# A state-space, token-mixing and MLP kernel on one core: the same steps issued in another order

## The chip, the core and the metric

The kernel runs on one core of a Trainium2 chip. A core has five engines that run their own instruction streams in order and meet at semaphores: PE (TensorE, matmuls; its weight loads are listed apart as PEld), DVE (VectorE), ACT (ScalarE), POOL (GpSimd) and SP (SyncE, which here only issues DMAs). Sixteen DMA engines serve the core. The metric is the device time of one execution in microseconds, the median of several runs.

## The reference

With x of 2048 x 512, the output is x plus a long convolution gated by an MLP block. Both branches see the same normalised input.

```python
xn = _layernorm(x, axis=-1)
s = _A_ref(xn, A_A_re, ..., A_log_dt, A_Dskip)      # state-space convolution
g = _silu(_B_ref(xn, B_w1, B_w2, B_w3, B_w4))       # token mixing and MLP
return x + s * g

# _A_ref: a kernel of length 2048 for each of 512 channels, from 128 complex states,
# and the convolution with it by Fourier transforms
P = jnp.exp(logdA[:, :, None] * l[None, None, :])
K = jnp.einsum("dn,dnl,dn->dl", Cc, P, dB).real
Yf = Uf * Kf[None, :, :, :]
y = ... + u * Dskip[None, None, :]

# _B_ref: four quarters of the channels shifted by +1, -1, +2, -2 tokens, then the MLP
h = _gelu(_layernorm(x, axis=-1) @ w1)
hs = jnp.concatenate([g0, g1, g2, g3], axis=-1) @ w2
x1 = x + hs
h2 = _gelu(_layernorm(x1, axis=-1) @ w3) @ w4
return x1 + h2
```

The shapes are L = 2048, D = 512, 128 states and an inner MLP width F = 1376.

## The kernel before

**How the work is staged.** X stays on the chip as sixteen slices of 128 tokens x 512 channels. The stages, with the names of their tiles, are these.

- *Start.* X is loaded in five pieces (x0 is slices 0 and 1, x1 is 2 and 3, then three of four slices), each in four transfers by rows. 40 matmuls on the identity (`ident`) run while nothing else is there. DVE and ACT normalise X (`stats`, `mv`, `rs`, `bs`).
- *Token mixing.* Eight pairs of slices are normalised once more (`x2`), transposed (`xT`, on TensorE for the first four pairs, by a transposing DMA of float16 halves `x2h` for the rest), multiplied with w1 (`h_pair`, h0 to h7, into `pb`) and passed through gelu (`hT`). `hs_pair` multiplies with w2 and adds to X. The same X goes through the first step of the Fourier transform (`u_stage1`, `ue`), and its result to DRAM (`scr_Ud`).
- *Weights.* w3 and w4 are loaded twice (`wst`): once for a sum of squares that sets a scale, once to be split in two float16 halves (`w3h`, `w4h`).
- *Tables.* The convolution's kernel is built in sixteen chunks of 32 channels (`phases`, `waves`, `factors`, `sums`): magnitudes and phases by Exp and Sin on ACT, products on DVE (`wv`), 64 small matmuls (into `pc`), a copy `kev`, the first transform step (ks0 to ks15, copies `k1e`), and two stores to DRAM a chunk, `scr_Kfa` for chunks 0 to 7 and `scr_Kfb` for 8 to 15.
- *MLP.* Eight blocks of two slices, each in six pieces: matmuls with `w3h` (groups of 12, 128x256), gelu to `g`, split to float16 halves `ghl`, matmuls with `w4h` (groups of 6, 128x512). These groups have no deadline but the end, and the order uses them to fill TensorE while other chains run.
- *Products.* In two halves of the channels (0 and 1), each step loads matrices `cst`, the input's transform `uin` and the kernel's `kin`, multiplies spectra (kspec, uspec), and goes through the inverse step (inv) to `z1e` and DRAM (`scr_Zda`, `scr_Zdb`). The second half does this in eight steps, with float16 halves `kx` and `uh`; step n loads its `cst` into the buffer that step n-2 used. The loads read all of a scratch array, so they wait for its last store.
- *End.* Eight gates (Silu on X) and, for each half, eight inverse steps (`zin0.0` to `zin0.7`, `zin1.0` to `zin1.7`): load `zin`, matmuls into `pc` and `pd`, DVE multiplies them into X, adds the input `xr`, and stores. zin0.3 loads into the buffer of zin0.0, zin0.6 into that of zin0.3.

**What sets the order.** The functions do not issue anything. Every operation is recorded as a step with its dependencies (`Plan.add`, or `Plan.together` for a group of matmuls), 1952 in all. Then `Plan.order` reads a list that is written out in the source, `ORDER`, and `Plan.issue` emits the steps in it, all from one line (330), which is why every row of the profile has that line and is told apart by its tiles. Since each engine runs its stream in order, the list fixes the order on each engine, SP's DMA issues among them (some DMAs are issued by ACT, as the X loads and stores by rows). A step that is a plain copy or a scale and bias (`Either.copy`, `Either.affine`) may run on ACT or on DVE: its number then ends in `a` or `v`. There are 370 of these.

```python
def order(self):
    out = []
    for word in ORDER.split():
        op = self.ops[int(word.rstrip("av"))]
        op.eng = {"a": "ACT", "v": "DVE"}.get(word[-1]) or list(op.alts)[0]
        op.cost, op.calls = op.alts[op.eng]
        out.append(op)
    place = {op.idx: k for k, op in enumerate(out)}
    assert len(place) == len(out) == len(self.ops)
    assert all(place[d] < place[op.idx] for op in out for d in op.deps)
    return out
```

The compiler puts a load of a function set before an ACT operation whose function is not in the set that is loaded. In this kernel Exp, Sin, Gelu, Sqrt and Silu are in five sets, so the order on ACT also sets how often a set is loaded.

**Steps by number**, as they stand in the list: 5 to 8 are the loads of x0, 20 to 23 those of x1, 9 and 10 those of w1; 2 is the group of 40 identity matmuls; 142, 143, 145 and 146 are h0; 741 is ks7 and 1268 ks15; 849 and 1586 are the first spectrum products of either half; 1635, 1663, 1691, 1719, 1747 and 1775 load `cst` for steps 2 to 7 of the second half; 1799 is its last inverse and 1802 the last store to `scr_Zdb`; 1820 and 1841 are the matmuls of zin0.0 and zin0.3, 1840 the load between them; 1867 to 1869 are zin0.6; 1562 is the last MLP matmul group and 1563, 1564 its two updates of X.

Of the kernel before, what the change touches and what calls it, by code (L numbers as in the profile page):

```python
# [116 lines left out]
23 20 21 0 22 39 7 8 1 6 5 105 86 3 2 106 107 108 109 110 111 112 87 89 88 90 113 91 114 115a 92 93 94 95 25 24  # L117
26 27 116a 96 97a 1070 98v 117a 120v 99v 100 101a 102v 103 118 172 170 4 168 171 169 173 9 104a 10 19 18 11 28
166 167 174 175 176 121 123 124 177 178 122v 119a 125 145 44 179 180v 183v 146 46 126 127 128 181a 147 47 48
187a 208a 142 31 29 30 182v 129 78 205a 130 148 79a 153a 184v 228 229 230 131 143 160 185 35 34 33 32 132 232  # L120
133 149v 154a 231 144 186a 188 134 552 226 189a 233 193 150a 227 234 235 135 236 237 194 161 196 190 293 553 295
294 291 238 14 292 297 155 156 13 16 15 191 239 298 296 138a 240 299 244v 300 140a 301 202a 242a 302 141 554
241v 303 201a 49 245v 50 209 195 206 52 51 304 246a 247 53 54 192 152 17 151 380 382 203 249a 214 207a 250a 197a
198a 305 215 211 212 12 199 204 200 157 251 139 56 216 55 210a 59 45 80 217 243v 57 555 381 307a 272a 213 383 58
60 253 254 306a 81a 61 164 218a 62 36 252 223a 219a 384 248 308v 273v 222a 158 63 274 255 67 268v 162 68 64 256
257 220 225 259 276 221 224 275 565 277 314v 269a 69 270 70 136 137 71 557 258 65 261a 260a 279 265a 315v 278 66
264a 316 388 309v 72 280 282 73 271 337v 310a 311v 74 84 312 262 263 281 284v 283v 318 75 560 562 319 333v 317
266 267 338v 287a 76 339 313 288a 77 321 322 85v 334v 323 324 335 285 286 42 82 586 558 320 344 83a 345 556 385
559 566 567 340 326a 325a 289 346 389 336 341 290 330a 329v 43 37 328 327 568 359 360 587 561 347 588 331 349v
571 159 348v 40 332 163 353v 352v 350 351 361 375 378 446 374 570 448 390 342 355 569 377 572 449 563 564 362  # L130
354 41 363v 394 592 468 450 364a 589 438 591 386 590 391 470 471 396 439 574 573 440 343 576 575 387 443 454 577
578 595 593 165 441 579a 395 367a 397 392 356 376 357 456 455 400 402 607 393 594 404 608 442 358 366 398 457
580 472 581 582a 583a 597 459 584 403 596 613 372 609 401 447 368a 369 451 399 416 610 611 460 598 452 599 405
417 444 365 406 371 435 418 585 612 600a 628 370 616 629 458 630 469 473 419 474 601 38 407 475 453 462 432 614
631 633 632 480 495 602 420 408 603a 604a 461 615 409 634 421 410 445 411 379 499 476 605 606 657 412 618 422
413 477 617 478 414 373 482 423 637 424 479 425 494 481 463a 544a 635 433a 545a 464 415 619 620 502 621a 485
548a 549a 546 636 622 426 491 434 649 428 550 436a 650 496 659 660 547 465 466a 503 517 516 437 639 654 521 651
504 661 638 430 551 467 653 652 492a 746 623 747 488 489a 518 507 624a 490 662 748 510 493 655 513 749a 861 753
524 511a 750 754 760 512 761 755 756a 751 775 776 640 641 752 656 486 757 625a 767a 768a 427 769 514a 525a 663
515 527 526 664 528a 762 771a 763a 529 429 770 530 642a 533 764 500 643 683 777 782 758 531a 665 532 684 626 627  # L140
772a 773 783 784 534a 774 658 759 778a 779 789 765 766 644 780 796 797 685 535 668 483 666 671 667 669 670 790
785a 791a 786 645a 686 798 673 646a 792 688 672 687 803 689 505 781 804 846 648 692 810 787 674 675 704 676a 805
677 431 647 811 788 678 793 847 812 799a 817a 705 679a 690 806a 706 825 795 800 794 680a 707 818a 709 832 826
691 807 693 801 802 808 809 694 813a 814 821a 822a 695 696 713 681 819 708 823 827 828a 725 726 820 501 727 710
829 711 824 815 833 697a 834 698 839 816 728 835a 840 1273 830 1274 699 682 712 714 731 730 836 700a 841a 715
842 729 732 734 733 701a 1280 703 1281 831 837 838 716 1275 717 1282 1079 1071 1276v 718a 719 735 1277 1072 736
1302 1287 843 484 845 1294a 1081 1283a 702 844 1284 1080 1073 1076 720 721a 722a 724 723 1288 737 738 1278 1279
1285 1303 1075 1106 1082 1295a 1298a 739a 1296 1074 740 1077 1084 1083 1078 1085 487 1289 1304 1086 1290a 1291
741 851 1286 1305v 1299v 742a 743a 1107 1087 1088 1300 1093 1090 1089 1297 1316 1309 1310 497 1306 1292 1293
1307 1308 506 1108 1091 1092 1317 1311 1312a 1109 1111 744 1301 745 1330 1323 1331 1313 1095 1094 862 1112 508  # L150
1314 1318a 498 848 849 850a 852 1110 509 853 860 536 1096 1097 1324 854 855 1113 856 1315 1098a 857a 858a 865
863 1319 1325 1326a 1128 537 538 876 1114 1115 875 859 889 1332 864a 866 868 867 869 890 1320 1099 1327 1116
1117 539 1352 1337 1338 874 1100 870 871a 1101 872a 1102a 877 1103a 1344a 878a 1322 1321 873 888 904 879 903
1129 1105 1333a 1345a 1339 1130 1346 1347 880 1131 882 1118 881 883 1119 1353 1334 1104 1354 1134 1328 1329 1133
884 885a 1132 1335 1150 886v 1359 1137 1151 1340a 1152 891 893 917 1366 1336 1341 887 902 1135 1120a 1348a 1342
1360 1153 892a 894 1121 895 1349a 1155 1122 896 897 1355a 898 899a 900a 918 916 1136 1350 1123 905 1124a 906a
907 1343 1138 1125a 1154 1356 908 1357 901 909 911 910 1351 1139 1361 912 1140 1141 1367 913a 1126 919 1142a 931
1156 920a 914v 1157 1143 1159 930 915 1144 1362a 921 1172 922 1373 1374 1173 923 1358 1180 1174 924 1176 925
1158 1127 1177 1175 1368v 1369 1178 1179 926 932 927a 928a 1145 929 1182 933 1363 945 946 935 934a 936 937 939
938 1380 1381 1161 1364 1365 940 1370 1185 1183 1184 1375 1376a 1181 1194 1186 941a 1394v 1160 944 1146a 942a  # L160
1382 1387 947 943 949 1383a 948a 1147a 1187 950 1377 959 952 958 973 974 1388 1162 1163 1188 951 953 1389 1191
1395v 522 1371 1372 1207 954 1409 955a 956a 1396 1190 960 957 1384 1164a 1398a 1189 1148 972 1397 1208 961 963
962v 964 965 966 1209 1378 1402 1379 1390a 967 1165 1391 1403 1385 1166 968 1399a 1192 1193 1400 1149 969a 970a
988 1210 1167 975 976a 977 978 980 979 986 1410 1386 1168a 981 1169a 971 1170 1195 987 1001 1211 1212 1404 1405a
1196 1213 1392 1393 523 982 1197 1198 984a 991 983a 1401 1171 985 1000 1216 989 1199a 990a 1002 1406 1229 1230
1407 1416 1200 1201 1417 1408 992 993 1231 1430 995 1411 1431 1423 1424 1214 1412a 994 996 1235 1014 1232 1015
1418a 1016 1202 1215 1218 998a 1425 1413 1005 1217 997a 999 1203a 1204a 1432 1419 1238 1205 1003 1004a 1006 1008
1219 1220 1007 1251 1233 1234 1414 1009 1444v 1415 1010 1028 1012a 1011a 1013 1206 1252 1221v 1029 1452 1253
1017 1222 1236 1019 1420 1018a 1437 1020 1022 1021 1254 1223 1224 1256 1023 1426a 1024 1030 1422 1026a 1043
1025a 1237 1421 1027 1427 1225a 1226a 1240 1227 1044 1228 1239 1433a 1453 1438 1445a 1042 1033 1031 1032a 1057  # L170
1260 1446 1034 1255 1241 1242 1434 1035 1243a 1244 1036 1428 1245 1429 1257 1037 1439 1435 1246 1038 1058 1258
1259 1247a 1454 1248a 1448a 1040a 1447 1039a 1056 1459 1466 1261 1262 1440a 1250 1045 1047 1046v 1048 1041 1263
1264 1049 1441 1265a 1050 1051 1460 1449v 1266 1052 1267 1268 1450 1053a 1059 1249 1461 1054v 1269v 1270v 519
1060v 1061 1062 1436 1608 1580 1455a 1063 1456 1442 1443 1457 1064 1065 1451 1804 1055 1467 1610v 1271 1066
1067a 1458 1272 1582v 1565 1566 520 1462v 1567 1463 1568 1611 1583 1811 540 541 1473 1474 1569 1464 1480 1579
1570 1571 1465 1572 1573 1574 1576 1578 1581 1068a 1475 1577 1476a 542 1575 1468a 1584v 1609 1069 1481 1612a
1692 1607 1482 1637 1590 1585 1586 1636 1665 1469 1613 543 1664 1470 1587a 1487 1588a 1589v 1591 1592 1693 1471
1596 1600 1472 1597a 1598a 1477 1599a 1601 1483a 1602 1640a 1488 1593 1614 1595a 1484 1818 1615a 1594v 1616a
1617a 1618 1638a 1478 1641 1603 1813 1604a 1489 1619 1605v 1639 1635 1624 1625a 1626a 1628 1666a 1885 1627a
# [1179 lines left out]
```

## Time and profile before

| | |
|---|---|
| time, median of 3 runs | 536.88 us (535.10 to 538.08) |
| the profiled execution, its span | 536.6 us |
| granted TensorE clock, mean | 0.994 |
| instructions | 13619 |

The profile's times are those of one execution of 536.6 us. A windows row splits the span into stretches, and the stages stand in them roughly like this: start to 13 us, token mixing to 100, first tables and MLP to 248, first products, second tables and MLP to 380, the last tables to 421, second products, gates and first inverse steps to 518, and the end. A row of the timeline has the start, the busy time, the engine, the operation with output and inputs, the shapes, how many instructions are put together, and in brackets how long the engine stood idle before and what released it. In the chain of waits each row is start, length, and what the time was spent on.

### The profile page before, as it was taken

What the parts mean: (1) busy time and instruction counts of PE and PEld (TensorE: products, weight loads), DVE (VectorE), ACT (ScalarE), POOL (GpSimd) and SP (SyncE); (2) the same over time, 40 slices, a digit from 0 to 9 for tenths busy, and PEclk for the clock granted to TensorE, in tenths of its full rate; (3) what the DMA queues carried; (4) which work ended last, traced back from release to release, by engine and by line L of the source; (5) the groups of instructions that cost most, each with busy time, mean ns of one, the idle gap of its engine ahead of it and who ended that gap; (6) DMA issues with size and microseconds to landing.
All of it is one profiled execution on the core that took longest, in us unless ns stands there. A gap on an engine that the chain in (4) does not pass through costs nothing.

```text
span 536.6 us, 13619 instructions
## 1 busy us (share of the span) xinstructions
PE 516.5 (96%) x5628; PEld 332.4 (62%) x5628; DVE 489.8 (91%) x755; ACT 425.2 (79%) x692; POOL 0.7 (0%) x6
## 2 busy tenths in 40 slices
PE   8999999999999999999999999999899899999992
PEld 7787664554475766565765666575565667666631
DVE  4999999999999999999999999999877799997277
ACT  3999999899899999999799897868646566774340
POOL 0000000000000000000000000000000000000000
PEclk9999999999999999999999999999999999999997
DMA  8989975689677325356375738838889969896997
GB/s 228 214 268 257 230 200 155 190 132 127 158 188 118 46 36 60 42 68 112 120 137 148 150 108 167 145 94 176 149 170 169 348 201 297 261 280 226 314 277 205
DMA packets 212830, 93.50 MB, mean 174 GB/s; under 512 B 163297, under 2 KB 196065, under 8 KB 212385
## 3 DMA queue, kind: packets, MB, share of 16 engines
q1 hardware_dynamic: 208032, 88.18, 71.3%
q10 hardware_dynamic: 4736, 4.46, 2.8%
q8 instruction: 44, 0.72, 0.6%
q14 instruction: 18, 0.14, 0.1%
HBM read 56.96 MB, written 29.36 MB: 161 GB/s over the span
## 4 chain that ended last, share of the span: by engine, by line
PE 63%; DVE 12%; ACT 11%; DMA 7%; issue 3%; SPq 1%; DVEq 0%; ACTq 0%
PE pb L330 24%; PE pa L330 17%; PE pd L330 11%; PE pc L330 11%; DVE wv L330 4%; DMA scr_Kfb<-k1e 3%; DVE X L330 3%; ACT wv L330 2%; ACT mag L330 2%; ACT L330 2%; SPq L330 1%; DMA kin<-scr_Kfb 1%; DMA scr_Kfa<-k1e 1%; DMA cst<-c_gq 1%; ACT g L330 1%
## 5 line engine op out<-in xcount | busy, mean ns | idle before, releaser
L330 PE MATMUL pb<-x1T,w3h 128*128 128x256 f16 (+1 forms) x1056 | 125.1, 273 | 1.2 <-ACT g L330 1.2
L330 PE MATMUL pa<-w4h,ghl 128*128 128x512 f16 (+1 forms) x528 | 123.2, 380 | 0.0
L330 PEld LDWEIGHTS <-w3h 128*128 128x128 f16 (+1 forms) x1056 | 102.3, 100 | 27.8 <-issue 11.0
L330 PEld LDWEIGHTS <-ghl 128*128 128x128 f16 (+1 forms) x528 | 49.3, 98 | 59.1 <-issue 8.7
L330 ACT ACT_TABLE_LOAD x52 | 66.7, 1283 | 2.0 <-PEq L1347 1.2
L330 ACT ACTIVATE wv<-wv 128x2080 f32<-128x2080 int32 x32 | 63.0, 1968 | 0.3 <-DVE wv L330 0.3
L330 ACT ACTIVATE g<-pb,wsc 128x512 f32<-128x512 f32 (+1 forms) x48 | 30.6, 651 | 12.8 <-PE pb L330 11.5
L330 ACT ACTIVATE ghl<-g,wsc 128x512 f16<-128x512 f32 (+1 forms) x39 | 26.6, 688 | 13.3 <-PE pa L330 8.3
L330 DVE TENSOR_TENSOR wv<-wv,eg 128x2048 f32<-128x2048 f32 x16 | 36.5, 2284 | 0.1
L330 DVE TENSOR_TENSOR wv<-mag,wv 128x2048 f32<-128x2048 f32 x16 | 36.6, 2285 | 0.0
L330 PE MATMUL pd<-pr,cst 64*128 64x256 f32 x256 | 36.3, 402 | 0.0
L330 PEld LDWEIGHTS pc<-wv 128*32 128x32 f32 x2048 | 29.8, 109 | 9.7 <-issue 6.2
L330 PE MATMUL pc<-wv 128*32 128x64 f32 x2048 | 32.5, 220 | 2.7 <-issue 1.9
L330 DVE SCALAR_TENSOR_TENSOR ghl<-g,wsc,ghl 128x512 f16<-128x512 f32 (+1 forms) x48 | 33.5, 701 | 1.0 <-ACT ghl L330 0.8
L330 ACT ACTIVATE wv<-wv,halfpi 128x2080 f32<-128x2080 f32 x16 | 32.9, 2056 | 0.1
L330 ACT ACTIVATE mag<-par 128x128 f32<-128x128 f32 x132 | 32.8, 441 | 0.0
L330 ACT ACTIVATE kh<-pc,ksc 128x256 f32<-128x256 f32 (+1 forms) x40 | 20.1, 553 | 14.1 <-PE pc L330 12.5
L330 PEld LDWEIGHTS pd<-pr,cst 64*128 64x128 f32 x256 | 22.0, 186 | 11.5 <-issue 8.3
L330 PE MATMUL pb<-xT,w 128*128 128x256 f32 x128 | 29.0, 382 | 0.0
L330 PEld LDWEIGHTS pb<-xT,w 128*128 128x128 f32 x128 | 23.8, 190 | 5.5 <-issue 1.6
L330 PE MATMUL pb<-w,hT 128*128 128x512 f32 x58 | 26.9, 599 | 0.0
L330 DVE BATCH_NORM_STATS2 stats<-X 128x6 f32<-128x512 f32 x32 | 21.4, 681 | 5.3 <-DMA X<-in_A_u_dram 5.3
(167 smaller groups left out, 882.7 us busy)
## 6 DMA issues: line engine op xcount, KB each, us to landing
wst<-in_B_w_dram SPq DMA_DIRECT2D x20, 512.0 KB, 4.0
scr_Ud<-ue SPq DMA_DIRECT2D x32, 256.0 KB, 3.2
scr_Kfa<-k1e SPq DMA_DIRECT2D x16, 256.0 KB, 6.2
uin<-scr_Ud SPq DMA_DIRECT2D x16, 256.0 KB, 4.1
cst<-c_gp SPq DMA_DIRECT2D x16, 256.0 KB, 3.5
kin<-scr_Kfa SPq DMA_DIRECT2D x16, 256.0 KB, 3.6
scr_Zda<-z1e SPq DMA_DIRECT2D x16, 256.0 KB, 3.0
scr_Kfb<-k1e SPq DMA_DIRECT2D x16, 256.0 KB, 6.0
```

The source lines that it names most:

```text
L330: ins = [getattr(self.engines[op.eng], name)(*args, **kw).ins for name, args, kw in op.calls]
```

## The change

Only the string `ORDER` differs: 82 of its lines are replaced by 78. It holds the same 1952 numbers, so the steps, their shapes, buffers and PSUM banks are the same; their place differs, and 116 of the 370 steps that may run on either engine change it, 59 from DVE to ACT and 57 from ACT to DVE. The beginning and the end of the two lists:

```diff
 ORDER = """
-23 20 21 0 22 39 7 8 1 6 5 105 86 3 2 106 107 108 109 110 111 112 87 89 88 90 113 91 114 115a 92 93 94 95 25 24
-26 27 116a 96 97a 1070 98v 117a 120v 99v 100 101a 102v 103 118 172 170 4 168 171 169 173 9 104a 10 19 18 11 28
...
-1867 1871 1861 1899 1862 1864 1563 1564 1868 1845 1869 1831 1810 1865 1872 1873 1896 1898 1846 1897 1900 1874
-1943 1909 1877 1875 1902 1901 1910 1911 1876 1878 1903 1863 1913 1922 1905 1907 1914 1915 1924 1923 1916 1904
-1906 1917 1919 1918 1920 1926 1935 1936 1937 1927 1928 1938 1940 1939 1941 1929 1942 1944 1945 1930 1931 1932
-1946 1947 1950 1951 1948 1933 1949
+0 7 3 2 5 8 6 89 23 87 88 19 44 90 91 92 93 22 20 21 105 107 94 95 108 96 98v 24 106 109 9 97a 110 39 99a 111 100 102v
+103 27 112 10 101a 113 114 115v 117v 118 104a 142 143 116a 119a 26 120v 121 86 25 170 123 124 1 166 172 125 4 126 34
...
+1828 1899 1563 1810 1896 1898 1871 1921 1847 1925 1897 1909 1872 1865 1873 1864 1943 1911 1874 1848 1875 1900 1902
+1878 1901 1913 1910 1903 1922 1924 1876 1914 1915 1926 1906 1907 1846 1923 1863 1935 1916 1862 1917 1927 1937 1877
+1919 1920 1905 1904 1936 1928 1944 1938 1942 1939 1940 1929 1941 1918 1930 1931 1933 1932 1946 1945 1947 1948 1949
+1950 1951
```

Counted in the two lists, in the stretches that are spoken of below:

| | before | after |
|---|---|---|
| x0's four loads | behind x1's four | ahead of them |
| MLP matmul groups ahead of table chunk 2 / 8 / 15 | 0 / 67 / 123 | 16 / 84 / 139 |
| MLP groups between ks7 and the first product of half 0 | 13 | 10 |
| MLP groups in the release of `cst` to its use, steps 2, 3, 4, 7 of half 1 | 3, 2, 2, 2 | 2, 2, 1, 1 |
| MLP groups between zin0.0 and zin0.3 | 5 | 3 |
| MLP groups between the last inverse of half 1 and zin1.0 | 21 | 11 |
| zin0.6's matmuls (1867) | behind the last MLP group (1562) | ahead of it |
| function-set loads on ACT | 52 | 57 |

More of the change, by code (lines that the diff above doesn't have):

```diff
@@ L122 @@
[L122 to L136, printed above, removed]
```

133 lines of the change are left out of this document (72 added, 61 removed).

## The prediction

> **What bounds the kernel now.** I read the page's first lines first, then the windows by stage, the list of what TensorE waited for, and last the rows of the places where it waited. The order alone changes, so the question is which waits a new order can remove, and which it makes.
>
> ```profile
> span 536.6 us, 13619 instructions
> PE 516.5 (96%) x5628; PEld 332.4 (62%) x5628; DVE 489.8 (91%) x755; ACT 425.2 (79%) x692; POOL 0.7 (0%) x6
> ```
> ```profile
> 100.00:248.00 148.00, 146.03 (x1643) 88.00 (x1641) 145.34 (x198) 140.23 (x225) 0.00 (x0) 1.00 0.64 107
> 248.00:380.00 132.00, 131.31 (x1666) 84.38 (x1669) 130.98 (x167) 111.24 (x180) 0.00 (x0) 1.00 0.62 136
> 380.00:421.00 41.00, 37.75 (x494) 23.51 (x483) 30.74 (x57) 22.86 (x34) 0.00 (x0) 1.00 1.03 195
> 421.00:518.00 97.00, 96.91 (x940) 63.95 (x937) 78.47 (x112) 59.62 (x98) 0.00 (x0) 1.00 0.88 272
> 518.00:536.60 18.60, 8.40 (x164) 2.83 (x162) 13.96 (x28) 1.06 (x1) 0.00 (x0) 0.83 0.76 211
> ```
> ```profile
> PE pc L330 <- issue: 1.9, 1, 1.9
> PE pc L330 <- DVE kx L330: 1.4, 2, 1.0
> PE pa L330 <- POOL ident masks.py:199: 1.4, 1, 1.4
> PE pd L330 <- DVE x L330: 1.3, 1, 1.3
> PE pb L330 <- ACT g L330: 1.2, 2, 0.7
> PE pc L330 <- ACT k1e L330: 0.9, 1, 0.9
> PE pc L330 <- DVE kev L330: 0.6, 1, 0.6
> ```
>
> The first fence is the page, the second the windows, the third what PE waited for (us in total, times, longest). A window row gives the stretch, its length, then busy time of PE, PEld, DVE, ACT and POOL, the granted clock, the DMA share and GB/s. TensorE (PE) is busy 516.5 of 536.6 us; the other 20.1 us are all there is to win, and some 10 of them are the tail from 518 on, where DVE finishes the output. TensorE's work is the same 1952 steps, so the floor is near 517 plus a start and a tail. DVE is as full as TensorE up to 380 (145.34 of 148, 130.98 of 132): its results come just in time. From 421 to 518 TensorE has no hole (96.91 of 97.0), while the DMA engines are busy 0.88 of the time. There anything that comes late is paid in full.
>
> **The change part by part.** Same steps; I count what stands between two steps in either list and price it by this profile's rows.
>
> Start, **-1.3**. The new list issues x0's four loads ahead of x1's four (the old one has them behind), so 512 KB less stand before the first transposes.
>
> ```profile
> 0.00:13.40 13.40, 10.78 (x80) 10.59 (x80) 6.25 (x27) 4.72 (x8) 0.70 (x6) 1.00 0.88 228
> ```
> ```profile
> 1.35 10.78 PE L330 MATMUL pa<-ident 128*128 128x128 f32 x80 [1.35 <-POOL ident masks.py:199]
> ...
> 13.45 1.09 PE L330 MATMUL pd<-ident,x 128*128 128x128 f32 x8 [1.31 <-DVE x L330]
> ```
>
> At 228 GB/s, 512 KB is 2.3 us. The transposes now start at 13.45; the warm-up matmuls on the same engine end at 1.35 + 10.78 = 12.13, so only 1.3 of the 2.3 count. Bounds: nothing (the normalisation on DVE and ACT then sets the start) to 2.4, if h0, which now follows three transposes and not four, also moves up.
>
> Waits in the first 380 us, **-1.0 and -2.7**. Around 66 us, ahead of the eighth projection (h7), the weight loads wait 1.9 us.
>
> ```profile
> PEld pd L330 <- ACT ue L330: 1.1, 2, 0.8
> PEld pc L330 <- DVE x2h L330: 0.8, 1, 0.8
> ```
>
> They wait for a chain from h3 through x2h and the transposing DMA to h7. TensorE work between its source and its use grows from 19.2 to 20.5 us: I take 1.0 off (0 to 1.9). In the table chunks the waits for k1e, kev and g are 0.9 + 0.6 + 1.2 = 2.7. The new list has far more MLP work ahead of each chunk's matmuls: groups of MLP matmuls ahead of chunk 2 go from 0 to 16, of chunk 8 from 67 to 84, of chunk 15 from 123 to 139. TensorE's work ahead of chunk 8, less DVE's work ahead of what it needs, goes from 248.3 - 240.0 to 273.7 - 253.9, from 8 to 20 us of lead. So all 2.7 goes. The other end is 0: the lead is real only if DVE isn't held up by the MLP's own halves.
>
> The hole of 1.9 marked "issue" waits for nothing the trace shows. I take half, **-0.9** (0 to 1.9).
>
> In the tail zin0.6's matmuls and its two multiplies move ahead of the last MLP update.
>
> ```profile
> 519.47 0.74 DVE L330 TENSOR_TENSOR X<-X,pd 128x256 f32<-128x256 f32 x2
> 519.59 1.06 ACT L330 ACTIVATE X<-X 128x1024 f32<-128x1024 f32 x1 [4.84 <-DVE X L330]
> ```
>
> DVE is the chain there: two multiplies (0.74) leave it, and those of zin1.0, which don't need the last Silu (1.06 on ACT), fill its wait. DVE's steps behind the update fall from 26 to 24, by such rows from 12.4 to 11.7 us: **-0.65** (0 to -1.2).
>
> Now what gets worse. **Last stage: the constants.** Each product step loads its matrices (cst, 512 KB) into a buffer that the inverse matmuls two steps before set free.
>
> ```profile
> 431.75 0.34 SPq L330 DMA_DIRECT2D cst<-c_gq  x1
> ...
> 437.21 0.58 PEld L330 LDWEIGHTS <-cst 128*64 128x64 f16 x12 [0.37 <-DMA cst<-c_gq]
> ```
> ```profile
> PEld L330 <- DMA cst<-c_gq: 0.9, 3, 0.4
> ```
> ```profile
> cst<-c_gq SPq DMA_DIRECT2D x1, 512.0 KB, 5.4
> ...
> cst<-c_gq SPq DMA_DIRECT2D x1, 512.0 KB, 3.6
> ```
> ```profile
> 422.57 1.31 PE pb L330 x12
> ```
>
> The loads for steps 2 to 7 landed after 5.4, 3.6, 4.9, 4.9, 4.5 and 3.6 us (the DMA view of each stretch; the first and the last of the six stand above). Between release and use the old list has 5.3 to 5.4 us of TensorE work, and the load was needed the moment it came (437.21 is 5.46 after 431.75): three of the six uses waited for it with their weight load, 0.9 in all. The new list has one MLP group of 12 matmuls (1.31) or one inverse fewer in four of them: 4.2, 4.2, 4.0, 5.4, 5.3 and 3.5 us. With 0.25 from release to issue and from landing to use, the stalls are 5.65 - 4.2, nothing, 5.15 - 4.0, nothing, nothing, 3.85 - 3.5: **+2.95**. Bounds: every load at 3.6 gives 0.35, every one at 5.4 gives 1.45 + 1.45 + 1.65 + 0.25 + 0.35 + 2.15 = 7.3. The Trainium skill, SBUF — State Buffer, section "The DMA setup-cost knee", fits a transfer by some 2 us and its bytes at 436 GB/s, an estimate of 3.2 us for 512 KB; no run here shows one under 3.5, and by it this term were nothing and the sum 2.95 lower.
>
> **zin0.3.** Its load takes the buffer that zin0.0's matmuls free; TensorE work between them falls from 7.2 to 4.8 us (two MLP groups fewer).
>
> ```profile
> zin<-scr_Zda SPq DMA_DIRECT2D x1, 512.0 KB, 3.5
> ```
> ```profile
> zin<-scr_Zda SPq DMA_DIRECT2D x7, 512.0 KB, 6.4
> ```
>
> At 3.5 us, this load's own, nothing is late; at 6.4, the median of seven in this stage, 1.85 is. The new place is nearer to the last scr_Zdb store and its reloads, so half: **+0.9**.
>
> **Turnarounds through DRAM.** Behind the first half's last table chunk (ks7) stand 10 MLP groups before its spectrum needs them, not 13: 13.1 us of cover, not 16.7. Behind ks15 the cover goes from 19.0 to 18.3.
>
> ```profile
> 400.96 0.13 DVE k1e L330
> ...
> 402.93 9.37 DMA scr_Kfb<-k1e
> ...
> 412.35 5.86 DMA kin<-scr_Kfb
> ```
> ```profile
> scr_Kfa<-k1e SPq DMA_DIRECT2D x16, 256.0 KB, 6.2
> kin<-scr_Kfa SPq DMA_DIRECT2D x16, 256.0 KB, 3.6
> ```
>
> For ks7 that is copies and issue 1.9 (400.96 to 402.93), store 6.2, load 0.5 + 3.6: 12.2, under 13.1; with the 9.37 and 5.86 of the other half 17.6, 4.5 over. I take **+1.0**, nearer to its own rows (0 to 4.5). ks15 waits today (kx, 1.4), so 0.7 less cover is **+0.7** (0 to 1.4). The losses sum to +5.55.
>
> **Engines and function sets.** 116 copies change engine (59 to ACT, 57 to DVE): no net work moves. Changes of the array's form between neighbouring matmuls fall from 188 to 182; none has a row of its own, and by the nearest, 12 weight loads in 0.58 at 437.21, six are worth 6 x 0.05: **-0.2** (0 to -0.3). With that the gains sum to -6.75. ACT's function-set loads, counted in the list, go from 52 to 57.
>
> ```profile
> L330 ACT ACT_TABLE_LOAD x52 | 66.7, 1283 | 2.0 <-PEq L1347 1.2
> ```
>
> That is 5 x 1.283 = 6.4 us more on an engine that idles 111 us: priced at nothing, with the lead above as cover.
>
> The stage from 421 also gets shorter for the same traffic: from its first product to the end TensorE's work falls from 106.2 to 85.2 us, and the lists' transfers only from 30.3 to 28.8 MB. At 272 GB/s (0.88 share, so some 309 at full share) that is 93 us in about 95. I charge no more than the two loads above, but it is why they may land late.
>
> **Sum.** -6.75 + 5.55 = -1.2, span 536.6 to 535.4. The median of the runs, 536.88, is 0.28 over the profiled span: **535.7**.
>
> **The rivals.**
> **A, faster**: the loads land as their fastest did (3.5 and 3.6) and the turnarounds stay covered. The losses shrink to 0.35: 536.88 - 6.75 + 0.35 = 530.5. For it: half of the load rows. Against: three loads at 4.9 and over, at a lower share of DMA than is to come. The page's rule above speaks for A.
> **B, slower**: the constants' loads all land at 5.4 and zin0.3's at 6.4, since the transfers of the last stage crowd. 7.3 + 1.85 + 1.0 + 0.7 - 6.75 = +4.1: 541.0; with ks7's 4.5 as well, 544.5. It decides at a mean landing of about 5.2 us: from there each 0.1 us costs 0.6, and the sum passes +2.7.
> **C, moved waits**: DVE, full to 380, doesn't run ahead as counted, and the waits of 2.7, 1.0 and 0.9 come back elsewhere: 535.7 + 4.6 = 540.3. For it: DVE at 98% in those windows. Against: the lists' lead.
> **D, function sets**: the five loads fall where TensorE waits for a g, as twice today (1.2 us), each in full: 535.7 + 6.4 = 542.1. For it: those two waits. Against: ACT's 111 us. The Trainium skill, ScalarE: Activation LUTs, section "What ACT_TABLE_LOAD costs", gives a load of 1283 ns, as the row does, and 1380 ns of draining besides, which would make 13.3 us of the five. The row's idle time, 2.0 us before 52 loads, doesn't show such a drain.
>
> **How the numbers follow.** Forecast 0.40 (its own range 533 to 538: one quarter of it under 534.2); A 0.26; C 0.12; B 0.18; D 0.04. A measurement of this kernel tells some 0.5%, 2.7 us, from no change: 534.2 to 539.6. Faster: 0.10 + 0.26 = 0.36. Same: 0.30 and parts of C (0.06) and B (0.04), 0.40. Slower: 0.06 + 0.14 + 0.04 = 0.24. The range runs from A's time, 530.5, to 542.0, between B's two times and about D's; it leaves out about 2 in 10.
>
> **What would show it.** Start: transposes at 12.1, no wait for x. Chunks: no wait for kev, k1e or g between 100 and 380, and chunk 8 standing further back in time. Last stage: in place of 96.91 of 97.0, TensorE waits for cst in four places and perhaps for zin; a wait named kin or for the spectrum's copies behind ks7. It is wrong if TensorE waits for DVE between 100 and 380 as much as today, if cst lands in under 4 us throughout (A), or if a wait appears in the weight preparation or for ACT behind a function-set load.

## The result and the profile after

The changed kernel is **slower**: 563.21 us (median, 558.40 to 566.49) against 537.48 for the kernel before (with a fourth run added to the three above), a ratio of 1.046 (95% interval 1.040 to 1.053). The forecast was 535.7 with a range to 542.0, so even the range missed it, by 21 us.

The page of the changed kernel (its steps are all issued from line 326):

```profile
span 561.9 us, 13611 instructions
...
PE 524.5 (93%) x5628; PEld 337.7 (60%) x5628; DVE 494.2 (88%) x753; ACT 431.4 (77%) x699; POOL 0.7 (0%) x6
```

TensorE does the same 5628 matmuls in 8.0 us more (524.5 for 516.5) and is not busy for 37.4 us, where it was 20.1. The sum is the 25.3 us by which the span grew. To find where, I split both executions at one event: the issue of the last store of the last table chunk, ks15 (402.9 us before, 428.9 after). The windows of the kernel before, then of the changed one (length, then busy PE, PEld, DVE, ACT, POOL, granted clock, DMA share, GB/s):

```profile
0.00:100.00 100.00, 96.14 (x744) 69.70 (x745) 90.27 (x197) 90.16 (x159) 0.70 (x6) 1.00 0.82 214
100.00:402.90 302.90, 298.35 (x3668) 185.51 (x3666) 295.00 (x390) 262.82 (x421) 0.00 (x0) 1.00 0.65 124
402.90:536.60 133.70, 122.04 (x1219) 77.16 (x1217) 104.48 (x170) 72.19 (x113) 0.00 (x0) 0.98 0.91 258
```
```profile
0.00:100.00 100.00, 93.94 (x619) 68.73 (x620) 81.75 (x186) 79.45 (x148) 0.70 (x6) 1.00 0.78 203
100.00:428.90 328.90, 323.98 (x3950) 204.15 (x3949) 317.93 (x423) 292.41 (x449) 0.00 (x0) 0.99 0.60 117
428.90:561.90 133.00, 106.53 (x1061) 64.83 (x1059) 94.52 (x146) 59.58 (x103) 0.00 (x0) 0.89 0.90 260
```

This is the main reading of the case, from one profiled execution of each kernel. **Everything up to ks15's stores takes 26.0 us longer, and everything behind them only 0.7 us less.** The new order moved 16 groups of MLP matmuls from behind that point to ahead of it. Ahead of it, TensorE's busy time rises by 23.4 us (394.5 to 417.9) and DVE's by 14.4 (385.3 to 399.7), in a part where both were nearly full: before the change, from 100 us on, TensorE was busy 98.5% and DVE 97.4% of the time. The 417.9 us of TensorE's work alone are 15.0 more than the 402.9 that the whole part took before, so at least 15.0 of the 26.0 us follow from TensorE's work there. Behind the store TensorE has 15.5 us less to do and DVE 10.0, and it takes as long as before: TensorE waits instead, 26.5 us not busy for 11.7. The DMA columns are nearly the same. 133.7 us at 258 GB/s and 133.0 at 260 are 34.5 and 34.6 MB: the same bytes at the same rate, at a share of 0.91 and 0.90.

What TensorE waited for in the changed kernel, the longest of the list:

```profile
PE pc L326 <- DMA cst<-c_gq: 7.9, 4, 4.1
PE pd L326 <- DMA zin<-scr_Zda: 3.7, 1, 3.7
PE pc L326 <- DMA zin<-scr_Zdb: 3.2, 2, 2.0
PE pd L326 <- ACT xT L326: 2.5, 2, 2.2
PE pd L326 <- DVE z1e L326: 2.1, 1, 2.1
...
PE pc L326 <- ACT k1e L326: 0.6, 1, 0.6
PE pd L326 <- issue: 0.6, 1, 0.6
...
PE pb L326 <- ACT g L326: 0.2, 1, 0.2
```

Before, this list had mostly DVE and ACT tiles in it. Its longest row, which the prediction's list leaves out, belongs to the tail:

```profile
PE pc L330 <- DVE X L330: 3.6, 4, 1.5
```

Now the first three rows, 14.8 us together, are waits for loads of the last stage. The chain of waits shows the first of them:

```profile
428.90 9.37 DMA scr_Kfb<-k1e
...
439.20 7.80 DMA cst<-c_gq
447.00 0.04 issue
447.05 2.77 PE pc L326 x24
```
```profile
445.44 1.28 DVE L326 SCALAR_TENSOR_TENSOR kx<-kin,ksc,kx 128x1024 f16<-128x1024 f32 x1 [6.37 <-ACT kx L326]
...
447.05 1.28 PE L326 MATMUL pc<-kx,cst 128*64 128x256 f16 x10 [4.07 <-DMA cst<-c_gq]
```

The load of `cst` for step 0 of the second half (step 1579) waits for nothing itself, but in the new list it stands in SP's queue behind the loads of `kin`, and these wait for ks15's last store to land. So it goes out at 439.2, and TensorE stands for 4.07 us. The second fence, the timeline, warns of the next one: the copy `kx` that the same matmuls need ends at 446.72 (445.44 + 1.28), and the load lands at 447.00 (439.20 + 7.80), only 0.3 us later. The load is named because it came last, not because it stood alone.

The list of DMA issues, by stretch, has two more slow loads of the stage; the timeline has where they were waited for:

```profile
cst<-c_gq SPq DMA_DIRECT2D x1, 512.0 KB, 7.5
...
zin<-scr_Zda SPq DMA_DIRECT2D x1, 512.0 KB, 10.1
```
```profile
499.93 0.84 PE L326 MATMUL pc<-kx,cst 128*64 128x256 f16 x12 [2.46 <-DMA cst<-c_gq]
...
523.03 0.64 PE L326 MATMUL pd<-zin,is 64*32 64x256 f32 x16
523.34 0.36 SPq L326 DMA_DIRECT2D zin<-scr_Zda  x1
...
533.55 1.11 PE L326 MATMUL pd<-zin,is 64*32 64x256 f32 x16 [3.67 <-DMA zin<-scr_Zda]
```

The load issued at 523.34 for zin0.6 landed after 10.1 us, and the matmuls at 533.55 had waited 3.67. Look at their length too: 16 matmuls take 0.64 us at 523.03 and 1.11 at 533.55, behind the wait. The granted clock of the last part fell from 0.98 to 0.89, and of the 8.0 us of longer busy time 6.3 lie in the groups of matmuls on `kin`, `uin`, `kx`, `uh` and `zin` (0.9, 0.8, 1.0, 1.4 and 2.2 us more, by the rows of the costliest groups). The first two groups stand ahead of ks15's stores, the other three, with 4.6 us, behind them.

### The profile page after: what moved, and what is told of

Same layout as the page of the kernel before. It is cut to its first block, busy times and chain, and to the rows that moved or that the text cites. A ratio compares the mean times of both kernels' runs of the same rounds, so it can differ in the third digit from the quotient of the medians.

```text
span 561.9 us, 13611 instructions
## 1 busy us (share of the span) xinstructions
PE 524.5 (93%) x5628; PEld 337.7 (60%) x5628; DVE 494.2 (88%) x753; ACT 431.4 (77%) x699; POOL 0.7 (0%) x6
## 4 chain that ended last, share of the span: by engine, by line
PE 53%; DMA 21%; DVE 12%; ACT 8%; SPq 2%; issue 2%; POOLq 0%; ACTq 0%; POOL 0%; DVEq 0%
PE pb L326 19%; PE pa L326 16%; PE pd L326 9%; PE pc L326 8%; DVE wv L326 6%; DMA cst<-c_gq 4%; DMA scr_Kfb<-k1e 3%; DMA scr_Kfa<-k1e 3%; DMA zin<-scr_Zda 3%; SPq L326 2%; DMA X<-in_A_u_dram 2%; DMA scr_Zda<-z1e 2%; DMA scr_Ud<-ue 2%; DVE ghl L326 1%; ACT wv L326 1%
## 5 line engine op out<-in xcount | busy, mean ns | idle before, releaser
L326 PE MATMUL pb<-x1T,w3h 128*128 128x256 f16 (+1 forms) x1056 | 123.4, 273 | 0.3 <-ACT g L326 0.2
L326 ACT ACT_TABLE_LOAD x57 | 73.1, 1283 | 6.1 <-DVE ghl L326 3.5
L326 ACT ACTIVATE kh<-pc,ksc 128x256 f32<-128x256 f32 (+1 forms) x39 | 19.3, 550 | 22.8 <-PE pc L326 14.1
L326 DVE SCALAR_TENSOR_TENSOR ghl<-g,wsc,ghl 128x512 f16<-128x512 f32 (+1 forms) x48 | 33.3, 699 | 1.2 <-ACT ghl L326 1.1
L326 ACT COPY z1e<-pd 128x256 f32<-128x256 f32 x56 | 18.9, 376 | 19.3 <-PE pd L326 13.4
L326 PEld LDWEIGHTS <-cst 128*64 128x64 f16 x384 | 20.9, 117 | 15.8 <-DMA cst<-c_gq 9.9
L326 ACT ACTIVATE ghl<-g,wsc 128x512 f16<-128x512 f32 (+1 forms) x34 | 22.7, 675 | 5.4 <-DMA xr<-in_A_u_dram 5.0
```

The source lines that it names most:

```text
L326: ins = [getattr(self.engines[op.eng], name)(*args, **kw).ins for name, args, kw in op.calls]
```

## The experiments

One idea was to be tested against another. Theory 1: the new order moved work into a part that was full, and the last stage has another limit than TensorE (its transfers), so it could not give the time back. Theory 2: the last stage is still set by TensorE's work, and the time was lost at single bad places of the new list. Ratios are to the kernel before, run on the same chip. A difference to the changed kernel is the difference of the two ratios times 538 us, and its uncertainty the root of the squares of the two intervals. The changed kernel's own interval is 3.6 us to either side, so few of these differences are sharp.

**Splices of the two lists.** The first four runs tried to take the lists apart.

```diff
 e1  ORDER = before, its MLP steps placed as in the new list
 e2  ORDER = new, its MLP steps placed as in the list before
 e3  ORDER = new up to step 577 (its first 437 steps), then the rest as before
 e4  ORDER = new up to step 1799 (its first 1808 steps), then the rest as before
```

> The list before, with the order and the engines of every step outside the MLP left as they were; only the MLP's steps stand where the new list has them among TensorE's other steps (140 instead of 124 of its 176 matmul groups ahead of ks15, 11 instead of 21 behind the last inverse). Theory 1 (cover: the new list spends its MLP groups early, and the last stage's transfers then have too little matmul work over them): most of the loss appears, 550 to 562 us. Theory 2 (queues: the new places of DMAs, copies and single steps in the last stage make them late, whatever the MLP does): near before, 535 to 541 us.

> The new list, with every step outside the MLP in its new order and on its new engine; only the MLP's steps go back to where the list before has them among TensorE's other steps (124 groups ahead of ks15, 21 behind the last inverse). Theory 1 (cover): most of the loss goes, 538 to 546 us, the rest being the new start and the first products. Theory 2 (queues): it stays, 555 to 565 us.

e1 took 723.35 us, a ratio of 1.336 (1.326 to 1.346), and e2 694.45, 1.285 (1.276 to 1.294). Both theories missed by over 100 us: TensorE waits for tiles all through e1, 20.6 us for `g` and 17.0 for `pr`. The likely reason, not tested, is that MLP steps put in by their place in one list stand across the chains of the other on every engine. They decide nothing between the theories.

> The new list up to the first matmuls of the first table chunk (some 107 us), then the rest in the order before. Both theories put the loss of the start at 2 us (TensorE had lost 5.3 us there in the new trace, 3.3 in the one before), so 537 to 541 us. If the start matters for what comes behind it (tables and weights late), over 544.

e3: 555.24 us, 1.024 (1.016 to 1.033), far over the 537 to 541 that both theories gave. At the seam TensorE waits 9.6 us for one `kev`. Up to 100 us it is idle 5.6 us, where it was 3.9 before, so the new start itself loses some 2 us. The stages behind the seam are little worse than before: from 125 us to ks15's last store TensorE is idle 6.5 us, where it was 4.0 from 110 us on. Since the seam alone makes so much, the run doesn't tell whether a late start makes later stages late.

> The new list up to the last inverse of the second half (513 us in its trace), then what is left in the order before. MLP groups behind that place are the same 11. Theory 1 (cover): the reloads and the last transfers are as crowded, 559 to 565 us. Theory 2 (queues): the 10 us that the new end loses over the one before go, 551 to 555 us.

e4: 560.62 us, 1.036 (1.029 to 1.042), 5.7 ± 5.1 us under the changed kernel. The time lies in Theory 1's range, but taken from the changed kernel's 563.2 by the ratios it is 557.5, between the two ranges; the run decides little. The old order of the end doesn't bring the whole loss back: its waits for the `cst` and `zin` loads are still there (8.6 and 6.7 us).

**Taking cover away from the kernel before.** If TensorE sets the last stage, less work there must shorten it.

```diff
+    CUT = {(6, 5), (6, 6), (6, 7), (7, 4), (7, 5), (7, 6), (7, 7), (7, 8)}
-                    for k in range(4):
-                        for lw, lx in ((0, 0), (0, 1), (1, 0)):
+                    for k in range(1 if cut else 4):
+                        for lw, lx in ((0, 0), (0, 1), (1, 0))[: 1 if cut else 3]:
...
+                            if (i_g, j) in CUT and (lg or lw):
+                                continue
```

> The list before, with TensorE's work of 16 MLP matmul groups of the last stage cut short (6 between the first product of the second half and its last inverse, 10 behind that, as many as the new list has fewer there): the w3h groups keep 1 of 12 matmuls, the w4h groups 2 of 6, so part of the MLP's sums is left out. Order, transfers and all other steps are the same. Work taken away: 8 x 1.2 + 8 x 0.86 = 16.5 us. Theory 1 (cover: with these groups gone the transfers of the last stage bind): TensorE waits for cst and zin there and the time falls by 0 to 6 us. Theory 2 (queues: only the new places of the other steps make them late): it falls by 15 to 17 us.

536.50 us, a ratio of 0.9935 (0.9905 to 0.9965): **16.5 us of TensorE's work taken away give 3.5 ± 1.6 us.** Its last part, in the windows:

```profile
405.10:534.60 129.50, 109.14 (x1095) 66.14 (x1093) 103.87 (x170) 71.35 (x113) 0.00 (x0) 0.95 0.94 267
```

Against 133.70 with 122.04 busy, TensorE now has 109.14, and the stretch is 4.2 us shorter at 267 GB/s. A wait for `zin<-scr_Zda` of 4.1 us and one for `cst` of 1.4 have come up in an order that is otherwise the old one. Theory 1's range held; Theory 2's 15 to 17 us is out. What the last part runs into when TensorE is relieved isn't transfers alone: in e5's chain of waits there, the loads of `xr` have 17.8% of the stretch, and DVE's products `pr` 9.6%.

**Less traffic.** Both orders without the transfers of the residual input (`xr`, about 4.2 MB in the last part); the last add takes X twice, so the output lacks the residual.

```diff
-            by_r(xr, xv[:, :, 4 * k : 4 * k + 4, ch], load=(Q, A))
+            by_r(xr[:, 0:1, 0:2], xv[:, :, 4 * k : 4 * k + 1, ch.start : ch.start + 2], load=(Q, A))
-        V.tensor_add(X[:, s0:s1, ch], X[:, s0:s1, ch], xr[:, s0 % 4 : s0 % 4 + s1 - s0])
+        V.tensor_add(X[:, s0:s1, ch], X[:, s0:s1, ch], X[:, s0:s1, ch])
```

> The list before; the 32 loads of the residual input (xr, 128 KB each, 4.2 MB in the last stage) shrink to 8 bytes a row, and the last add takes X twice, so the residual is left out. Both theories: no change within 1.5 us, as TensorE has no hole in that stage.

> The new list with the same cut: 4.2 of the 28.8 MB of its last stage are gone, 14 us at 300 GB/s. Theory 1 (cover): loads land sooner, 8 to 14 us less than the new list's time. Theory 2 (queues): 0 to 3 us less.

In the order before: 540.56 us, 1.000 (0.996 to 1.005), nothing. In the new one: 555.14, 1.027 (1.020 to 1.035), 10.2 ± 5.5 us less, in Theory 1's 8 to 14 and over Theory 2's 0 to 3. The last part of the new order without these loads:

```profile
427.10:551.70 124.60, 104.44 (x1063) 63.59 (x1060) 94.72 (x146) 59.63 (x103) 0.00 (x0) 0.91 0.83 244
```

133.0 us have become 124.6. So the same transfers cost nothing under the old order, whose MLP groups cover them, and are on the path in the new one. It isn't bandwidth alone: 4.2 MB at 260 GB/s would be 16 us, and 5.8 us of waits for `cst` remain in this run.

**Two loads moved.** The `cst` load of step 0 ahead of the `kin` loads, and two others behind step 1690 so that they stand out of the way (the lines are shortened to the steps around them).

```diff
-1505v 1664 1581 1498a 1609 1068a 1566 1499a 1579 1492
+1505v 1579 1664 1581 1498a 1609 1068a 1566 1499a 1492
...
-1527 1889 1819 1706a
+1527 1706a
...
-1747 1737v 1690 1733
+1747 1737v 1690 1819 1889 1733
```

> The new list with three DMA steps moved in SP's queue: the constants of the second half's first step (1579) go ahead of the loads that wait for ks15's stores, and two loads not needed soon (1819, 1889) go behind the constants of step 6 (1747), which landed after 7.5 us. Theory 2 (queues): the waits of 4.1 and 2.5 us at these two places go, 5 to 7 us less than the new list. Theory 1 (cover): the first is set by kin and kx, ready 0.4 us before the constants, and only step 6 gains, 1 to 3 us less.

561.26 us, 1.040 (1.034 to 1.046): 3.4 ± 4.9 us, unclear. What TensorE waited for:

```profile
PE pc L326 <- DMA cst<-c_gq: 5.2, 3, 2.3
...
PE pc L326 <- ACT kx L326: 2.8, 1, 2.8
```

The wait for `cst` falls by 2.7 us and a wait of 2.8 for `kx` stands in its place, as the 0.3 us in the timeline above had hinted. At the other place the wait of step 6 is gone, and step 7 waits 2.35 us instead. A removed wait is worth the distance to the next releaser.

**Filling the last stage.** 160 matmuls on the identity (ten a step, 21.3 us in all by their row; the text below has 80 of 0.27 us, about the same sum), put into the sixteen kernel-spectrum steps of the second half, into a bank that the real matmuls overwrite.

```diff
+                    for _ in range(5 * (bk is bank[2][0])):
+                        T.matmul(bk[:, :P], ident, ident, start=True, stop=True)
```

> The new list; each of the 16 first spectrum groups of the second half gets 5 more matmuls of the identity (128x128) ahead of its own, 80 in all at 0.27 us, so 21.6 us more TensorE work in the last stage, as much as the new list has fewer there. Theory 1 (cover: the transfers set the length of that stage): 0 to 6 us more than the new list, and less if a busier TensorE gets its clock back. Theory 2 (queues): 15 to 22 us more.

577.75 us, 1.074 (1.068 to 1.080): 14.8 ± 4.8 us more, so about 6.5 of the 21.3 are hidden, with the same uncertainty. Theory 1 had 0 to 6 and missed; the time agrees with Theory 2's 15 to 22. In the changed kernel only four of the eight steps waited for `cst`, so half of the fill stands at steps where nothing waited. The wait for `cst` is gone from TensorE's list (it was 7.9), but at step 0 a wait of 3.3 us for `g` stands in its place. So the stage isn't one long queue for transfers in which any work is free. A reading that fits, but that no run tests by itself, is a set of load loops, each of which hides only the work between its own release and use.

**The first part.** Does TensorE set it, or DVE? Three cuts in MLP blocks 1 and 2, which run ahead of ks15: matmuls alone (16.5 us), the second float16 half on DVE (5.6 us by its row, 33.3 to 27.7, and 9.5 us of matmuls that use it), and both, with some 45 us of matmuls by their count (32.8 us of busy time, at a lower granted clock).

```diff
 e10
+    CUT = {(i, j) for i in (1, 2) for j in range(4, 8)}
+                            if (i_g, j) in CUT and (lg or lw):
+                                continue
...    (and the loops over k and over the halves cut as in e5)
 e13
+    CUT = (1, 2)
+            q = slice(0, 8 if i_g in CUT else 2 * P)
-                ghl[:fr, 1, :n], g32[:fr, :n], sg[:fr], ghl[:fr, 0, :n], op0=ALU.mult, op1=ALU.subtract
+                ghl[:fr, 1, :n, q], g32[:fr, :n, q], sg[:fr], ghl[:fr, 0, :n, q], op0=ALU.mult, op1=ALU.subtract
+                            if i_g in CUT and lg:
+                                continue
 e14 (e13, and the loops over k and over the halves cut as in e5)
+                            if i_g in CUT and (lg or lw):
+                                continue
```

> The new list, with the same cut as in the run of before with less cover (8 w3h groups keep 1 of 12 matmuls, 8 w4h groups 2 of 6, so part of the MLP's sums is left out), but in blocks 1 and 2, at 170 to 240 us: 16.5 us of TensorE work less ahead of the last stage. Theory 1 says that the moved MLP work is paid where it went, since TensorE is full there: 10 to 16 us less than the new list. If DVE (97% busy there) is what fills that part: 0 to 5 us less.

> The new list; in MLP blocks 1 and 2 (170 to 250 us) the second float16 half of the gelu output is cut to 8 columns on DVE (12 steps of 0.7 us) and the w4h passes that read it are left out (2 of 6 matmuls, 9.5 us of TensorE work). If the first part is bound by DVE: 6 to 9 us less than the new list. If TensorE and DVE bind in turns: 2 to 5 us less. If neither: no change.

> The new list with that cut and with the w3h groups of blocks 1 and 2 at 1 of 12 matmuls and the w4h groups at 2 of 6, 45 us of TensorE work less. Bound by DVE: like the run before it, 6 to 9 us less than the new list, however much TensorE work goes. Bound by both in turns: 10 to 25 us less.

| | ratio | to the changed kernel, us | ks15's last store |
|---|---|---|---|
| e10, TensorE -16.5 | 1.050 (1.045 to 1.054) | +1.8 ± 4.4 | 425.9 |
| e13, DVE -5.6 | 1.038 (1.030 to 1.047) | -4.2 ± 5.7 | 424.2 |
| e14, both | 1.031 (1.027 to 1.036) | -8.0 ± 4.3 | 423.0 |

In the changed kernel and the runs with an unchanged first part that store stands at 426.2 to 429.8, so differences of 3 us are not to be read. What can be read is that 16.5 us less for TensorE give nothing, where Theory 1 had 10 to 16 us and a limit by DVE 0 to 5, and that the cut of both gives 8.0 ± 4.3, which fits a limit by DVE (6 to 9) and reaches that of both in turns (10 to 25) only with its edge. e13's 4.2 ± 5.7 tells nothing of the two. The window of e14 that holds most of the cut, and the same window of the changed kernel:

```profile
100.00:250.00 150.00, 122.05 (x1426) 68.34 (x1428) 145.66 (x211) 138.89 (x215) 0.00 (x0) 0.87 0.53 107
```
```profile
100.00:250.00 150.00, 149.34 (x1677) 92.40 (x1676) 147.82 (x208) 137.09 (x207) 0.00 (x0) 1.00 0.54 107
```

With TensorE at 122 of 150 us, DVE is at 145.66. So DVE, or the chain through it, holds that window. The whole part up to ks15's last store, in the kernel before, the changed kernel and e14, shows how much of the loss is left:

```profile
0.00:402.90 402.90, 394.50 (x4410) 255.22 (x4411) 385.27 (x586) 352.99 (x579) 0.70 (x6) 1.00 0.69 147
```
```profile
0.00:428.90 428.90, 417.93 (x4568) 272.88 (x4569) 399.68 (x608) 371.86 (x596) 0.70 (x6) 1.00 0.64 137
```
```profile
0.00:423.00 423.00, 385.16 (x4235) 246.13 (x4236) 393.50 (x606) 371.67 (x596) 0.70 (x6) 0.96 0.64 140
```

**In e14 TensorE has less to do in this part than it had before the change (385.2 us for 394.5), and the part still takes 20.1 us longer.** So the matmuls that moved in are enough for 15.0 us of the loss, but they aren't all that makes it: without them the new order of the first part, with 8.2 us more work for DVE and 18.7 more for ACT, is nearly as long. Two limits stand close together, and relief of one alone shows little.

**The third piece of X.** In the new list three of its four loads stand in SP's queue behind stores and weight loads.

```diff
-160 29 153a
+160 29 32 35 33 153a
```

> The new list; three of the four loads of X's third quarter (32, 33, 35), which stood in SP's queue behind the first stores to scr_Ud and two weight loads, go ahead of the parameters, right behind the loads of the second quarter. Both theories: the wait of 3 us at 45 us goes (TensorE's 2.2 for xT among it), 2 to 3 us less than the new list; nothing if the parameters that they now delay are as late.

559.55 us, 1.039 (1.032 to 1.045): 4.1 ± 4.9 us less, unclear as a time; but the trace moves with it. First the timeline of the changed kernel with those loads and what came of them, then the first 48 us of it and of e11 in the windows:

```profile
27.91 0.66 SPq L326 DMA_DIRECT2D X<-in_A_u_dram  x1
...
30.15 2.09 SPq L326 DMA_DIRECT2D X<-in_A_u_dram  x2
...
44.85 0.64 PE L326 MATMUL pd<-X,ks 32*64 32x512 f32 x1 [2.25 <-ACT xT L326]
```
```profile
0.00:48.00 48.00, 44.16 (x277) 36.52 (x278) 33.67 (x107) 32.19 (x55) 0.70 (x6) 1.00 0.92 237
```
```profile
0.00:48.00 48.00, 46.41 (x293) 38.76 (x294) 37.07 (x115) 35.63 (x60) 0.70 (x6) 1.00 0.94 244
```

By 48 us e11 has 3.4 us more of DVE's work done and 2.3 more of TensorE's; h7 starts at 70.9, which is 72.5 to 78.1 in the other runs that begin with the new list, and ks15's last store goes out at 424.1.

**The new start alone** (its first 56 steps, then the list before):

```diff
 e12 ORDER = new up to step 121, then the rest as before
```

> The new list up to the fourth transpose (56 steps, 15 us: x0's loads first), then the rest in the order before. The prediction's term for the start: 1.3 us less than before, transposes at 12.1 and not at 13.5 us; a seam as in the run with the new start up to the first table would cost more than that.

542.40 us, 1.008 (1.005 to 1.012). The transposes start at 11.86, 1.6 us earlier than before (13.45). But sixteen matmuls of the token mixing that started at 30.81 before now start at 35.33, 4.5 us later, so the seam costs some 6 us. A list is a weave for each engine, and a good beginning doesn't fit another's middle.

**A third buffer for the constants**, so that `cst` loads one step earlier; in `ORDER` each of these loads stands where the one before it stood (not shown):

```diff
-            uin=Ring(late, K4, 3), cst=Ring(late + 3 * K4, K4, 2), kin=Ring(late + 5 * K4, K4, 3),
+            uin=Ring(late, K4, 3), cst=Turns(late + 3 * K4, late + 4 * K4, early + 5 * K4), kin=Ring(late + 5 * K4, K4, 3),
```

> The new list with three buffers for the second half's constants in place of two, and each of their loads put where the load before it stood. If the two-buffer loop makes the waits: the 7.9 us for cst go but for the first, 4 to 7 us less than the new list. If crowded transfers make them: they move to other loads (zin, kin), 0 to 2 us less.

557.79 us, 1.035 (1.029 to 1.040): 6.3 ± 4.6 us less, in the range of a two-buffer loop (4 to 7), though the other range (0 to 2) is within the uncertainty. No wait for `cst` is left in its list. The wait at step 0 stands on as 3.65 us for `g`, and the `zin` waits remain. Its last part:

```profile
426.70:555.40 128.70, 105.48 (x1061) 63.90 (x1059) 94.28 (x146) 59.59 (x103) 0.00 (x0) 0.90 0.93 269
```

128.7 us, at 269 GB/s. That is 4.3 us less than in the changed kernel, of the 7.9 that `cst` had stood for. No version that does all the work beats the kernel before.

## Why the prediction was wrong

| term | forecast | what the runs show |
|---|---|---|
| start | -1.3 | transposes at 12.73 for 13.45, no wait for x: -0.7; X's third piece lost it again |
| h7 | -1.0 | its weight loads wait 2.1 us for x2h, as much as the 1.9 before: 0 |
| k1e, kev, g | -2.7 | 0.6 and 0.2 left, kev gone: -1.9 |
| hole "issue" | -0.9 | 0.6 left: -1.3 |
| tail, zin0.6 | -0.65 | its matmuls wait 3.67 for their load: +3.7 |
| cst, steps 2 to 7 | +2.95 | +3.8, but partly by luck: 2.46 of it at step 6, priced at nothing; steps 2 and 4 wait 0.95 and 0.42 for 1.45 and 1.15, step 7 not at all |
| cst, step 0 | not priced | +4.1, with kx ready only 0.3 us ahead of it |
| zin0.3 | +0.9 | about +0.5 |
| ks7 | +1.0 | 0.3 for kin |
| ks15 | +0.7 | no wait named kx; the 4.1 for cst stands at the same matmuls |
| form changes | -0.2 | no run shows this term; with its own 6 x 0.05 it would be -0.3 |
| function sets | 0 | 57 loads, no wait of TensorE behind them |
| first part, work moved in | not priced | +23.4 us of TensorE, +14.4 of DVE, +18.9 of ACT; the part is 26.0 us longer |
| last part, work moved out | not priced | -15.5 us of TensorE, only -0.7 us of time |

**The step that failed** is the one that reads, in the prediction, "The stage from 421 also gets shorter for the same traffic" and ends "I charge no more than the two loads above". The sum treated TensorE's 1952 steps as one pile: the same work, so the same floor near 517, and what is moved from the end to the beginning costs in one place what it saves in the other. It does cost in the beginning: of the +26.0 us up to ks15's stores, at least 15.0 follow from TensorE's work. It saves nothing at the end (-0.7), since there the MLP was cover for 34.5 MB of transfers and not the limit. e5 shows it from the other side: cover taken out of the old order is worth 3.5 us for 16.5.

A second step failed beside it: "no net work moves" for DVE and ACT is nearly true of the whole list (4.4 and 6.2 us more), but not of the first part, where DVE has 14.4 us more to do and ACT 18.9. e14 shows that the first part stays 20.1 us longer when more matmul work is taken out of it than had moved in.

The number that hid this was 309 GB/s, worked out as 272 at a share of 0.88, "93 us in about 95". No run came near it over the whole last part: the rate was 258 and 260 GB/s, and 267 and 269 in e5 and e15. 34.5 MB at 268 are 129 us, and e5, the changed kernel and e15 all took 128.7 to 133.0 for it. These rates are means of a stage and no ceiling that was shown: single slices of 13.4 us on the page before go up to 348 GB/s, and e7, with less to move, ran at 244. The prediction's own warning ("it is why they may land late") had the sign right and was given no price.

**Rival B**, late loads in the last stage, had the right mechanism for that stage, the wrong size, and nothing on the first part. It took every load at 5.4 or 6.4 us. As a rule the `cst` loads weren't later than that: those of steps 2 to 7 landed after 5.0, 4.0, 4.2, 4.0, 7.5 and 4.2 us, 4.8 on average, under the 5.2 at which B was to decide. Single ones were late, up to 7.5 (`cst`) and 10.1 (`zin`), and B knew only steps 2 to 7 and zin0.3, not step 0's load behind the `kin` loads in SP's queue, nor zin0.6, nor the `zin1` loads of the tail. Part of that is the queue itself. What SP's queue waited for, in the changed kernel:

```profile
SPq L326 <- DMA out_dram<-X: 9.2, 9, 4.1
...
SPq L326 <- DMA zin<-scr_Zda: 5.0, 4, 1.6
...
SPq L326 <- DMA zin<-scr_Zdb: 4.7, 3, 1.9
```

SP stood 18.9 us in these rows until earlier transfers had landed, before it went on. In the kernel before, the two rows of `zin` are 2.0 and 3.2 us, and there is none for `out_dram` from this line. A late load delays the next one's issue, and a sum that prices each load by its own landing misses that.

**Rival C** was right that waits would move: k1e, kev and g lost 1.9 us, and TensorE waits 2.1 for `z1e` in the first products instead. Behind this stands the larger matter that the lead counted from the list, 8 to 20 us ahead of chunk 8, was TensorE's lead over DVE, and it was bought by putting MLP work in front of both.

**Rival D**, as it was put, is out. The row of the function-set loads:

```profile
L326 ACT ACT_TABLE_LOAD x57 | 73.1, 1283 | 6.1 <-DVE ghl L326 3.5 <-PEq L1343 1.7
```

57 loads at 1283 ns, with 6.1 us of ACT's idle time ahead of them in all. TensorE waits for `g` 0.2 us in all, so no load stands in its way there. But the loads also moved: 52 of the 57 are issued ahead of ks15's last store, and 41 of the 52 before. That is 14.1 of ACT's 18.9 us more in the first part, and no run separates what it costs the chains of ACT and DVE. The drain of 1380 ns for each load in the Trainium skill, ScalarE: Activation LUTs, "What ACT_TABLE_LOAD costs", would be 79 us for 57, by estimate, and doesn't show in this row.

**What stays open.** How the 26.0 us of the first part divide. TensorE's work is enough for 15.0 of them, and the rest of the new order, with TensorE relieved, for 20.1, so the two overlap. By busy time DVE has 14.4 us more to do there and idles 11.6 more (8.5 of it in the first 100 us, where X's third piece comes late); TensorE has 23.4 more to do and idles 2.6 more. DVE's work, the eleven function-set loads on ACT and the late start are the candidates for the 20.1, and none was shown alone. e11 suggests that the late loads of X take part, but its 4.1 us is within its uncertainty. A list with the new order and the MLP put back, that would have shown the loss in one run, wasn't found: e2 broke the chains.

## What to carry to other kernels

Before work without a deadline is moved out of a stage, ask what else that stage needs time for; a first estimate is its bytes divided by the rate that was measured over that stage, not by a rate scaled to full share. A stage can't be shorter than the work of its fullest engine, so fill that goes into a stage where TensorE is full makes it longer (here by at least 15.0 us), and is paid back only where the stage it left was bound by that work. Less work for one engine shows nothing where a second one is as full. And follow each load in the queue that issues it: what stands ahead of it there and waits decides when it goes, and a wait that is removed is worth only the distance to the next one.

## What was not expected of the hardware

The granted clock falls where TensorE has short pauses. In the window of e14 above, where TensorE was busy 81% of the time, it was 0.87; and in the changed kernel's end:

```profile
520.00:545.00 25.00, 18.33 (x199) 7.72 (x198) 12.30 (x24) 11.04 (x12) 0.00 (x0) 0.86 0.96 267
545.00:561.90 16.90, 5.66 (x96) 1.91 (x80) 9.77 (x19) 0.00 (x0) 0.00 (x0) 0.52 0.90 286
```
```profile
L326 PE MATMUL pc<-zin,is 64*32 64x256 f32 x128 | 7.3, 477 | 5.7 <-DMA zin<-scr_Zdb 3.2 <-DVE X L326 1.8 <-DMA zin<-scr_Zda 0.8
```

A `zin` matmul took 477 ns on average, and 385 in the kernel before. So work that waits is also done more slowly afterwards, and a stall costs more than its length. The Trainium skill, TensorE: Matmul & The Clock Gate, section "Part 1: The HAM clock gate", has TensorE at half rate after an idle window of about 3.4 us. The 16 matmuls behind the wait of 3.67 us, 1.11 us for 0.64, agree with that. But in this trace shorter waits did it too, and the trace decides: behind a wait of 2.08 us, which ended at 334.10, and one of 2.46, which ended at 499.93, half the clock was granted, 0.51 and 0.50 in these windows:

```profile
333.90:337.40 3.50, 3.30 (x16) 1.71 (x16) 3.29 (x8) 3.50 (x17) 0.00 (x0) 0.51 0.60 203
```
```profile
501.30:504.60 3.30, 3.30 (x28) 2.26 (x26) 1.30 (x2) 0.94 (x3) 0.00 (x0) 0.50 0.33 65
```

The loads of `cst`, `zin` and `kin` behind ks15's stores, 512 KB each, landed after 3.5 to 8.5 us before and after 3.7 to 10.1 in the changed kernel, at nearly the same mean rate (258 and 260 GB/s). The estimate of 3.2 us by the Trainium skill, SBUF — State Buffer, "The DMA setup-cost knee", is that of a transfer alone; none of the `cst` and `zin` rows read here was as short.
